# One 128-row operand per head for the attention scores of a fused attention and mixture-of-experts kernel

## The chip, the cores and the metric

The program runs on one core of a Trainium2 chip. A core has a matrix engine (TensorE, PE in the profile, with its weight loads shown apart as PEld), a vector engine (DVE), an activation engine (ACT), a general engine (POOL), and a queue engine (SP) that here only issues DMAs. Each engine works through its own list of instructions in order, and semaphores tie the lists together. The metric is the device time of one execution in microseconds (us), less is better.

## The reference: what is computed

Attention with a decay comes first: 8 batches of 8 heads, 576 positions, 64 features a head. Then each of the 4608 tokens goes through one of 8 experts.

```python
scores = scale * np.matmul(q, k.transpose(0, 1, 3, 2))
cum = np.cumsum(np.log(np.clip(f, 0.0001, 1.0)), axis=-1)
scores = np.where(causal, -1e9, scores + cum[:, :, :, None] - cum[:, :, None, :])
attn = softmax(scores)                      # over the last axis
out = np.matmul(attn, v)                    # -> x, 4608 tokens of 512
e = argmax(x @ w_gate + modality_bias[modality_id])
y = gate_w * (relu(x @ w1[e]) @ w2[e])      # one expert of 8 for each token
```

Since `cum` of the query's row falls out of a softmax, a score needs q·k, minus `cum` of the key, minus a shift of the query (its maximum).

## The kernel before

**Attention.** The 64 heads are worked in 32 pairs `p`. A pair's operands stand together in one tile: the first head's 64 features in partitions 0 to 63, the second's in 64 to 127. To keep f32 accuracy, ACT rounds the loaded features to a shorter format (`split_hi`, L329) and POOL takes the rest (`split_lo`, L335): tile `X` holds both, for keys and queries.

A score group `scores(p, g)` is a sum in PSUM of five kinds of products: a mask (L480, a 128-row product of an identity and a triangle), high keys by high queries, high by low, low by high (all L492 from `X`), and a product of `Sk` and `Sq` (L492 as well), whose few live rows hold the negated cumulated logs of the keys and the shifts of the queries, high and low parts each. All but the mask have 64 rows: the first head's operands in the upper half, the second's in the lower, one matmul for each head, directly one after the other. The four groups of a pair are 288, 288, 448+64 and 320+192 columns wide.

Before that the shift is found. `max_mm` (L419 mask, L424 high by high, L428 `Sk` by the constant `Cq`) makes transposed scores in four groups, DVE reduces them to maxima (L438 to L443), PE transposes the maxima (L449), DVE splits them (L455, L456) and SP writes them into `Sq` with two DMAs (`shift_out`, L463). The logs come into `Sk` with one DMA (`put_cum`, L340). `Sk`, `Sq` and `X` have three buffers each.

Afterwards ACT takes the exponentials (L502) and rounds them (L513), POOL and DVE take the rest (L521), and PE multiplies by the values (`weighted`, L541 to L543, 45 small matmuls a head). DVE divides (L552 to L554), PE transposes (L568) and multiplies by the gate's weights (L584).

**What sets the order.** A class `Plan` orders all steps of the attention before anything is built. Each step has an engine, an assumed cost, the steps that it comes after, buffers that it takes and frees, and a due time: `PER` times its pair plus an entry of the table `DUE`. The planner goes through the steps by greedy choice, and each engine's list is its choice, fixed. The table is a list of numbers; the pairs are staggered by it, so that pair 18's maxima stand beside pair 16's scores. On SP the DMAs stand in one list in this order too.

**Experts.** The second half, from 512 us or so on, sorts tokens by expert and runs full-height matmuls of 128x256 and 128x512 (L1003, L1014); its code is not touched.

## Time and profile before

| what | us |
|---|---|
| median of three timed runs | 1025.76 (1023.96 to 1026.95) |
| the profiled execution | 1013.86 |
| its span, first to last instruction | 1012.1 |
| PE busy | 927.0 (92%) |
| DVE / ACT / POOL busy | 684.1 (68%) / 537.5 (53%) / 361.6 (36%) |

The profiled execution is one run, 1.76 us longer than its span; sums made on its rows are compared with its own time. A row of the timeline has the start and the duration in us, the engine, the source line, the operation with what it writes and reads, its shape (64*128 is a 64-row matmul that uses 128 columns of weights) and a count of merged instructions. Durations of matmuls overlap, so the pace is read from one row's start to the next row's start. A row of windows gives each engine's busy time in a stretch, then the clock granted to PE, as a share of full speed, and the DMA engines' busy share.

### The profile page before, as it was taken

The page shows a single profiled execution, that of the slowest core. Times are in us where ns is not written, and L with a number is a line of the kernel's source. Part 1 is how long each engine was busy: PE and PEld are TensorE (multiplying, and loading weights), DVE is VectorE, ACT ScalarE, POOL GpSimd, SP SyncE. Part 2 cuts the span into 40 slices and gives each one's busy share as a digit, 9 for nine tenths or more (in the row PEclk, how much of TensorE's full clock was granted, in tenths as well). Part 3 has the DMA queues.
Part 4 walks back from the last instruction along what each step waited for, and adds up shares of the span by engine and source line. Part 5 has one row for each costly group of instructions (what it writes and reads, how often), then busy time and mean ns, then how long its engine had stood idle before and what let it go on. Part 6 is the DMA issues. An engine that isn't in the chain of part 4 may idle for free. (4 is left out here: it accounts for less than half of the span.)

```text
span 1012.1 us, 22740 instructions
## 1 busy us (share of the span) xinstructions
PE 927.0 (92%) x9347; PEld 808.8 (80%) x9347; DVE 684.1 (68%) x1173; ACT 537.5 (53%) x655; POOL 361.6 (36%) x278
## 2 busy tenths in 40 slices
PE   5999989999999899979689999999999999999792
PEld 3787778777778777768588999999999999999571
DVE  7867978686777858777547766566666666665382
ACT  2765656655756547547443444445444544544371
POOL 7454556865566474653424311111111110111010
PEclk9897999998999969989779999999999999999796
DMA  5212132332321322212302676111111441124640
GB/s 180 77 50 99 33 126 67 99 99 74 97 78 53 99 84 89 87 57 86 131 33 79 218 256 235 43 43 42 53 43 53 134 139 55 43 84 168 234 161 3
DMA packets 38276, 98.22 MB, mean 97 GB/s; under 512 B 3919, under 2 KB 4559, under 8 KB 38160
## 3 DMA queue, kind: packets, MB, share of 16 engines
q1 hardware_dynamic: 31456, 75.60, 22.5%
q0 software_dynamic: 6704, 21.02, 5.5%
q8 instruction: 79, 1.29, 0.6%
q14 instruction: 37, 0.30, 0.1%
HBM read 133.69 MB, written 21.80 MB: 154 GB/s over the span
## 5 line engine op out<-in xcount | busy, mean ns | idle before, releaser
L521 POOL TENSOR_TENSOR Pl<-Pt,Ph 128x1152 f16<-128x1152 f32 (+1 forms) x64 | 152.3, 2385 | 156.2 <-ACT Ph L513 104.4
L502 ACT ACTIVATE Pt<-ps,lnp 128x1024 f32<-128x1024 f32 (+1 forms) x128 | 117.2, 928 | 112.8 <-PE ps L492 104.8
L1017 POOL DMA_INDIRECT out_dram<-y,xg x36 | 47.4, 1316 | 349.4 <-DVE y L1016 333.1
L1003 PE MATMUL ph<-xh,w1h 128*128 128x256 f32 x576 | 164.3, 286 | 2.0 <-ACT xh L991 1.5
L1003 PE MATMUL ph<-xl,w1h 128*128 128x256 f32 x576 | 164.3, 285 | 0.0
L1003 PE MATMUL ph<-xh,w1l 128*128 128x256 f32 x576 | 164.1, 285 | 0.0
L976 ACT CAST w2h<-raw 128x1024 fp32r<-128x1024 f32 x84 | 86.6, 1050 | 115.1 <-PE py L1014 84.7
L970 DVE TENSOR_TENSOR w1l<-raw,w1h 128x1024 fp32r<-128x1024 f32 x80 | 100.9, 1265 | 58.1 <-ACT w1h L969 57.7
L977 DVE TENSOR_TENSOR w2l<-raw,w2h 128x1024 fp32r<-128x1024 f32 x84 | 100.3, 1221 | 56.5 <-ACT w2h L976 55.2
L969 ACT CAST w1h<-raw 128x1024 fp32r<-128x1024 f32 x80 | 83.3, 1048 | 95.6 <-PE ph L1003 57.8
L492 PE MATMUL ps<-X 64*128 64x288 f32 (+4 forms) x1152 | 125.8, 327 | 0.0
L1014 PE MATMUL py<-w2h,hh 128*128 128x512 f32 x312 | 121.6, 398 | 0.0
L1014 PE MATMUL py<-w2l,hh 128*128 128x512 f32 x312 | 119.7, 391 | 0.7 <-DVE w2l L977 0.7
L1014 PE MATMUL py<-w2h,hl 128*128 128x512 f32 x312 | 119.5, 392 | 0.0
L513 ACT CAST Ph<-Pt 128x1024 f16<-128x1024 f32 (+1 forms) x96 | 103.7, 1082 | 21.3 <-PE po L543 20.3
L1003 PEld LDWEIGHTS ph<-xh,w1h 128*128 128x128 f32 x576 | 111.5, 194 | 3.6 <-ACT xh L991 2.4
L1003 PEld LDWEIGHTS ph<-xl,w1h 128*128 128x128 f32 x576 | 111.7, 194 | 0.7
L541 PE MATMUL po<-vh,Ph 128*128 128x65 f16 x960 | 104.9, 202 | 7.5 <-DVE x L554 7.5
L1003 PEld LDWEIGHTS ph<-xh,w1l 128*128 128x128 f32 x576 | 111.7, 194 | 0.0
L543 PE MATMUL po<-vh,Pl 128*128 128x65 f16 x960 | 104.7, 201 | 5.0 <-issue 3.5
L542 PE MATMUL po<-vl,Ph 128*128 128x64 f16 x960 | 104.8, 200 | 1.8 <-issue 1.8
L492 PEld LDWEIGHTS ps<-X 64*128 64x128 f32 x1152 | 93.1, 196 | 13.2 <-issue 1.8
(253 smaller groups left out, 2025.7 us busy)
## 6 DMA issues: line engine op xcount, KB each, us to landing
raw<-in_w_dram SPq DMA_DIRECT2D x84, 1024.0 KB
raw<-in_qk_dram SPq DMA_DIRECT2D x32, 608.0 KB
xg<-xs SPq DMA_DIRECT2D x20, 514.0 KB
vr<-in_v_dram SPq DMA_DIRECT2D x7, 1024.0 KB
raw1b<-in_w_dram SPq DMA_DIRECT2D x4, 1024.0 KB
hxg<-xs SPq DMA_DIRECT2D x5, 257.0 KB
vr<-in_v_dram SPq DMA_DIRECT2D x2, 512.0 KB
vr<-in_v_dram SPq DMA_DIRECT2D x8, 128.0 KB
```

The costliest lines, as they stand in the source:

```text
L492: nc.tensor.matmul(ps[:, h, c0:c0 + w], a, b, start=(j == 0 and not masked), stop=(j == 3), skip_group_check=True)
L502: nc.scalar.activation(self.get("Pt", (p, i))[:, :, o:o + w], ps[:, :, 0:w], AF.Exp, bias=self.lnp, scale=0.125)
L513: self.nc.scalar.copy(self.Ph_t[p % 2][:, :, c], self.get("Pt", (p, i))[:, :, 0:c.stop - c.start])
L521: e.tensor_tensor(self.Pl_t[p % 2][:, :, c], self.get("Pt", (p, i))[:, :, 0:c.stop - c.start], self.Ph_t[p % 2][:, :, c], ALU.subtract)
L541: nc.tensor.matmul(o, Ph[:, c0:c0 + P], vh[:, c, hh, :], start=(c == 0), stop=False)
L542: nc.tensor.matmul(o[:, 1:65], Ph[:, c0:c0 + P], vl[:, c, hh, :], start=False, stop=False)
L543: nc.tensor.matmul(o, Pl[:, c0:c0 + P], vh[:, c, hh, :], start=False, stop=(c == ic))
L970: nc.vector.tensor_tensor(self.w1l[a], self.raw1[i][a], f32(self.w1h[a]), ALU.subtract)
L976: nc.scalar.copy(self.w2h[a], self.raw2[a])
L977: nc.vector.tensor_tensor(self.w2l[a], self.raw2[a], f32(self.w2h[a]), ALU.subtract)
L1003: nc.tensor.matmul(ph[:, i, :], w[:, k, f0:f0 + P], x[:, k, :], start=(j == 0), stop=(j == len(m) - 1))
L1014: nc.tensor.matmul(py, h[:, k, c * P:c * P + P], w[:, k, :], start=(j == 0), stop=(j == len(m) - 1))
```

## The change

The rows of logs and shifts move into the operand itself. For each head `h` of a pair there is a 128-row operand `A[:, h, :]`: 64 rows are the head's rounded features (the same half of the partitions as before), the other 64 rows hold what stood in `Sk` and `Sq`: ones and cumulated logs on the key side, shifts and ones on the query side. One full-height matmul for each head then does high by high together with the logs and the shift. The two mixed products (high by low, low by high) stay 64-row matmuls. In `max_mm` the shift rows are still zero, and one full-height matmul for each head replaces both 64-row products.

The rounded features are made by ACT for both heads at once in a tile `H` (two copies of 576 columns in place of one of 1216), and go from `H` into the two heads' operands by two DMAs of 64x1280 (new step `cp`, function `put_hi`; for the first pair one ACT and one DVE copy). The logs take two DMAs, and from the fourth pair on two more set the shift rows back to zero; the shift takes four DMAs in place of two. A new function `blank` fills constants into three buffers of `A` at the start. `PER` and `DUE` are other numbers.

```diff
-PER = 13.5
+PER = 12.5
 DUE = {
-    ('setup2',): 36.45, ('hi',): -18.87, ('lo',): -67.23, ('cum',): -14.17, ('mm', 0): -2.46, ('mm', 1): -11.48,
+    ('setup2',): 33.79, ('hi',): -40.67, ('lo',): -86.81, ('cp',): -34.26, ('cum',): 31.87, ('mm', 0): 0.81,
...
+    def blank(self, i, e):
+        A = self.A_t[i]
+        self.nc.gpsimd.memset(f32(self.L_t[i][:, S:QC]), 0.0)
...
+        for h in range(2):
+            o, r = slice(64 - 64 * h, 128 - 64 * h), slice(64 * h, 64 * h + 64)
+            self.nc.gpsimd.memset(f32(A[o, h, S:QW]), 0.0)
+            self.nc.gpsimd.memset(f32(A[r, h, S:QC]), 0.0)
+            for c, m in ((slice(0, S), 0), (slice(QW, XW), 1)):
+                e.tensor_scalar(A[o, h, c], self.ones_f[o].broadcast_to([64, c.stop - c.start]), self.t01[m][o], None, ALU.mult)
...
     def split_hi(self, p):
-        X = self.new(self.qp, "X", p, [P, 2, XW], F32R, 3)
-        self.nc.scalar.copy(X[:, 0], self.get("raw", p))
+        H, raw = self.H_t[p % 2], self.get("raw", p)
+        self.own(("hi", p % 2), p)
+        for x, y in ((H[:, 0:S], raw[:, 0]), (H[:, QC:], raw[:, 1])):
+            self.nc.scalar.copy(x, y)
...
+    def put_hi(self, p):
...
+        H, A = self.H_t[p % 2], self.A_t[p % NX]
+        for h in range(2):
+            r = slice(64 * h, 64 * h + 64)
+            if p:
+                self.nc.sync.dma_start(f32(A[r, h]), f32(H[r]))
+            else:
+                (self.nc.scalar.copy, self.nc.vector.tensor_copy)[h](A[r, h], f32(H[r]))
 
     def put_cum(self, p):
-        self.nc.sync.dma_start(f32(self.Sk[16:P:32, p % 3, 0:S]), f32(self.chl[2 * p:2 * p + 2]))
+        for h in range(2):
+            o = 64 - 64 * h
+            self.nc.sync.dma_start(f32(A[o + 16:o + 64:32, h, 0:S]), f32(self.chl[2 * p + h:2 * p + h + 1]))
+            if p >= NX:
+                self.nc.sync.dma_start(f32(A[o:o + 64:32, h, QW:]), self.zrow)
...
     def max_mm(self, p, g):
-        for c0, w, ic, j0 in segs:
-            for h in range(2):
-                r = slice(64 * h, 64 * h + 64)
-                nc.tensor.matmul(pm[:, h, c0:c0 + w], X[r, 0, QC - 64 + P * ic:QC + 64 + P * ic], X[r, 0, j0:j0 + w],
-                                 start=not masked, stop=False, skip_group_check=True)
-            for h in range(2):
-                r = slice(64 * h, 64 * h + 64)
-                nc.tensor.matmul(pm[:, h, c0:c0 + w], self.Cq[r], self.Sk[r, p % 3, j0:j0 + w], start=False, stop=True,
-                                 skip_group_check=True)
+        for h in range(2):
+            for c0, w, ic, j0 in segs:
+                nc.tensor.matmul(pm[:, h, c0:c0 + w], A[:, h, QC - 64 + P * ic:QC + 64 + P * ic], A[:, h, j0:j0 + w],
+                                 start=not masked, stop=True, skip_group_check=True)
...
     def scores(self, p, g):
+        for h in range(2):
+            for c0, w, c, i0 in segs:
+                k, q = cols(c, w, i0)
+                nc.tensor.matmul(ps[:, h, c0:c0 + w], A[:, h, k], A[:, h, q], start=not masked, stop=False, skip_group_check=True)
         for c0, w, c, i0 in segs:
-            for j, (x, y) in enumerate(((0, 0), (0, 1), (1, 0), (2, 2))):
+            k, q = cols(c, w, i0)
+            for x in range(2):
                 for h in range(2):
                     r = slice(64 * h, 64 * h + 64)
-                    if x < 2:
-                        a, b = X[r, x, k], X[r, y, q]
-                    else:
-                        a, b = self.Sk[r, p % 3, k], self.Sq[r, p % 3, 64 + i0:64 + i0 + w]
-                    nc.tensor.matmul(ps[:, h, c0:c0 + w], a, b, start=(j == 0 and not masked), stop=(j == 3), skip_group_check=True)
+                    a, b = (A[r, h, k], L[r, q]) if x == 0 else (L[r, k], A[r, h, q])
+                    nc.tensor.matmul(ps[:, h, c0:c0 + w], a, b, start=False, stop=(x == 1), skip_group_check=True)
...
+            add("cp", k, "SP" if p else [("ACT", 1.2), ("DVE", 1.2)], 1.1, self.put_hi, k, [("hi", p)] + old, d - 2,
+                lands=655e3 if p else None)
```

Three places of the built lists show how instructions moved. A row has the source line, the operation, what is written and read, the output's size, and a count.

On PE, the maximum's last two groups of a pair (L424 reads the 64-row halves of `X`, L428 the 64-row `Sk`; L419 is the 128-row mask). Before:

```order
L424 MATMUL ps<-X 128x288 x2
L428 MATMUL ps<-Sk,Cq 128x288 x2
L419 LDWEIGHTS ident_162
L419 MATMUL ps<-after,ident_162 128x128
L419 LDWEIGHTS ident_162
L419 MATMUL ps<-after,ident_162 128x128
L424 MATMUL ps<-X 128x288 x2
L428 MATMUL ps<-Sk,Cq 128x288 x2
```

Now, in `max_mm` as well (L458 is the full-height product, L454 the mask, L396 a transpose that belongs to another step):

```order
L458 MATMUL ps<-A_159 128x288 x2
L454 LDWEIGHTS ident_175
L454 MATMUL ps<-after,ident_175 128x128
L454 LDWEIGHTS ident_175
L454 MATMUL ps<-after,ident_175 128x128
L458 MATMUL ps<-A_159 128x288 x2
L396 MATMUL pb<-ident,am 3x128
```

Four products each time became two, and every one of the rows is 128 high.

On PE, a score group of 288 columns. Before (L480 mask, L492 the four products of two heads, L362 another step's transpose):

```order
L480 LDWEIGHTS ident_162
L480 MATMUL ps<-later,ident_162 128x128
L480 LDWEIGHTS ident_162
L480 MATMUL ps<-later,ident_162 128x128
L492 MATMUL ps<-X 128x288 x6
L492 MATMUL ps<-Sq,Sk 128x288 x2
L362 MATMUL pb<-ident,am 3x128
```

Now (L511 mask, L517 full height, L524 the two 64-row kinds):

```order
L511 LDWEIGHTS ident_175
L511 MATMUL ps<-later,ident_175 128x128
L511 LDWEIGHTS ident_175
L511 MATMUL ps<-later,ident_175 128x128
L517 MATMUL ps<-A_159 128x288 x2
L524 MATMUL ps<-L_156,A_159 128x288 x2
L524 MATMUL ps<-A_159,L_156 128x288 x2
```

Eight matmuls became six, two of them full height, and the 64-row ones stand at the group's end.

On SP, one pair's share of the list in the middle of the attention. Before (features L325, logs L340, shifts L463):

```order
L340 DMA Sk<-chl 4x1x576
L325 DMA raw<-in_qk_dram 128x1216
L463 DMA Sq<-mT 2x5x128 x2
L340 DMA Sk<-chl 4x1x576
L325 DMA raw<-in_qk_dram 128x1216
```

Now (copies L362, logs L372, zeros L374, features L338, shifts L495):

```order
L362 DMA A_160<-H_153 64x1280 x2
L372 DMA A_160<-chl 2x1x576
L374 DMA A_160<-zrow 2x640
L372 DMA A_160<-chl 2x1x576
L374 DMA A_160<-zrow 2x640
L338 DMA raw<-in_qk_dram 128x1152
L495 DMA A_159<-mT 1x5x128 x4
L362 DMA A_158<-H_154 64x1280 x2
```

A pair's four DMAs became eleven, and the copy of a pair stands ahead of the shifts of the pair before it.

More of the change, by code (lines that the diff above doesn't have):

```diff
@@ L216, in setup @@
         make_identity(nc, self.ident)
[L217 to L218 removed]
+        self.H_t = [self.qp.tile([P, XW], F32R, name=f"H{i}") for i in range(2)]
+        self.L_t = [self.qp.tile([P, XW], F32R, name=f"L{i}") for i in range(NX)]
+        self.A_t = [self.qp.tile([P, 2, XW], F32R, name=f"A{i}") for i in range(NX)]
+        ones = self.ones_f = t([P, 1], F32, "ones_f")
         nc.gpsimd.memset(ones, 1.0)
[L220 to L225 removed]
+        self.t01 = t0, t1
+        self.zrow = t([2, QW], F32, "zrow")
+        nc.gpsimd.memset(self.zrow, 0.0)
+        self.blank(0, nc.vector)
         self.ident16 = t([P, P], BF16, "ident16")
@@ L458, in shift_out @@
     def shift_out(self, p):
-        self.own(("shift", p % 3), p)
-        mT = self.get("mT", p)
-        for a in range(2):
-            self.nc.sync.dma_start(f32(self.Sq[32 * a:P:64, p % 3, :]), f32(mT[:, a]))
+        self.own(("shift", p % NX), p)
+        mT, A = self.get("mT", p), self.A_t[p % NX]
+        for h in range(2):
+            for a in range(2):
+                r = 64 - 64 * h + 32 * a
+                self.nc.sync.dma_start(f32(A[r:r + 1, h, QW:]), f32(mT[NJ * h:NJ * h + NJ, a]))
     KSEG = [[(0, 288, 0, 0)], [(0, 288, 0, 288)], [(0, 448, 1, 128), (448, 64, 4, 512)], [(0, 320, 2, 256), (320, 192, 3, 384)]]
@@ L469, in scores @@
         nc = self.nc
-        X = self.get("X", p)
-        self.owned(("cum", p % 3), p)
-        self.owned(("shift", p % 3), p)
-        self.owned(("lo", p % 3), p)
+        L, A = self.L_t[p % NX], self.A_t[p % NX]
+        for x in ("cum", "A", "shift", "lo"):
+            self.owned((x, p % NX), p)
         ps = self.new(self.ps_s, "ps", (p, g), [P, 2, 512], F32, 3)
@@ L668, in steps @@
         n, nb = NH * self.nb // 2, self.nb
[L669 removed]
+        plan = Plan(dict(ps=3, pb=1, po=1, Pt=4, raw=2, mt=2, x=2, xT=2, sm=2))
         base = 0.0
```

67 lines of the change are left out of this document (33 added, 34 removed), and 20 rows, old and new, of the table DUE.

## The prediction, as it was put on record

> **What bounds the kernel now.** I read the granted clock and busy times by stage first, then PE's waits, then PE's timeline at full clock. The change touches only the attention, so its stage is what counts. The windows view (a stretch, its length, busy us and instruction counts of PE, PEld, DVE, ACT, POOL, then PE's clock, DMA share, GB/s):
>
> ```profile
> 50.00:500.00 450.00, 410.46 (x5951) 346.84 (x5948) 335.00 (x701) 274.54 (x329) 260.67 (x161) 0.92 0.26 85
> 250.00:300.00 50.00, 47.74 (x744) 40.51 (x743) 35.95 (x84) 33.76 (x40) 29.26 (x20) 1.00 0.27 87
> ```
>
> PE is busy 410.46 of 450 us (91%); DVE comes next with 335.00 (74%). The waits of PE in the same stretch (engine and tile, whom it waited for, total us, times, longest):
>
> ```profile
> PE pb L568 <- DVE lg L590: 9.2, 4, 5.9
> PE po L541 <- DVE x L554: 7.5, 5, 5.1
> PE pb L449 <- DVE roh L615: 4.8, 2, 3.1
> ```
>
> No engine holds PE regularly: these are a few long waits, 21.5 us of the 39.5 us that PE isn't busy, and none is for the shift's or the logs' DMAs. So PE's own list sets the pace, and what a step of PE costs there is paid nearly in full. A busy PE isn't a fast one, so I price by the steps from one row's start to the next. PE's timeline, a stretch at clock 1.00 (start, duration, what):
>
> ```profile
> 252.25 0.33 PE L419 MATMUL ps<-after,ident 128*128 128x64 bf16 x4
> ...
> 253.34 0.20 PE L541 MATMUL po<-vh,Ph 128*128 128x65 f16 x1
> ...
> 254.88 0.40 PE L424 MATMUL ps<-X 64*128 64x288 f32 x2
> 255.12 0.29 PE L428 MATMUL ps<-Sk,Cq 64*128 64x288 f32 x2
> 255.34 0.28 PE L419 MATMUL ps<-after,ident 128*128 128x128 bf16 x2
> 255.56 0.40 PE L424 MATMUL ps<-X 64*128 64x288 f32 x2
> ...
> 256.02 0.38 PE L377 MATMUL pb<-a,ones 1*128 1x1 f32 x2
> ...
> 259.57 0.20 PE L541 MATMUL po<-vh,Ph 128*128 128x65 f16 x1 [0.61 <-DVE x L554]
> ...
> 260.93 0.39 PE L419 MATMUL ps<-after,ident 128*128 128x128 bf16 x4
> 261.24 0.36 PE L424 MATMUL ps<-X 64*128 64x192 f32 x2
> ...
> 261.96 0.34 PE L480 MATMUL ps<-later,ident 128*128 128x128 bf16 x4
> ...
> 263.61 0.28 PE L480 MATMUL ps<-later,ident 128*128 128x128 bf16 x2
> 263.83 0.67 PE L492 MATMUL ps<-X 64*128 64x288 f32 x6
> 264.33 0.29 PE L492 MATMUL ps<-Sq,Sk 64*128 64x288 f32 x2
> 264.46 0.60 PE L492 MATMUL ps<-X 64*128 64x288 f32 x6
> 264.86 0.32 PE L492 MATMUL ps<-Sq,Sk 64*128 64x288 f32 x2
> 265.12 0.66 PE L568 MATMUL pb<-ident,x 128*128 128x128 f32 x4
> 265.61 0.39 PE L480 MATMUL ps<-later,ident 128*128 128x128 bf16 x4
> ...
> 267.14 0.34 PE L419 MATMUL ps<-after,ident 128*128 128x64 bf16 x4
> ```
>
> Two things are to be seen. First, two 64-row matmuls of the two heads run together: three pairs of 288 columns take 264.46 to 264.86, 0.133 us a pair. Second, going between 128-row and 64-row work costs extra, in three places. Into it: four masks take 0.31 us (260.93 to 261.24) and two take 0.22 (255.34 to 255.56), so a mask is 0.045 and the passage 0.13. At the first pair: three pairs right behind masks take 0.50 (263.83 to 264.33) instead of 0.40, so 0.10. Out of it: a pair followed by a 128-row instruction takes 0.22 (255.12 to 255.34) instead of 0.13, so 0.09. One 64-row block costs about 0.3 us beyond its products.
>
> **The change part by part.** *Maxima.* Now, for a pair of heads: 1.09 us (252.25 to 253.34), 1.14 (254.88 to 256.02) and 1.03 (260.93 to 261.96), in all 3.26. After the change everything there is 128 rows high. The trace has full-height matmuls of rounded f32 in the experts' half, each with new weights, and narrow ones at the gate:
>
> ```profile
> 599.93 0.28 PE L1003 MATMUL ph<-xh,w1l 128*128 128x256 f32 x1
> 600.05 0.28 PE L1003 MATMUL ph<-xh,w1h 128*128 128x256 f32 x1
> ...
> 605.45 0.39 PE L1014 MATMUL py<-w2l,hh 128*128 128x512 f32 x1
> 605.68 0.40 PE L1014 MATMUL py<-w2h,hl 128*128 128x512 f32 x1
> ```
>
> ```profile
> 483.89 1.26 PE L584 MATMUL pb<-wg,xT 128*128 128x8 f32 x10
> 485.01 0.38 PE L480 MATMUL ps<-later,ident 128*128 128x128 bf16 x4
> ```
>
> 256 columns take 0.12 us, 512 take 0.23; on that line 288 columns take 0.134, 320 0.148, 448 0.203. However narrow, a matmul with 128x128 f32 weights takes 0.11 (ten in 483.89 to 485.01), which I take for 192 and 64. A full-height matmul thus costs what a *pair* of 64-row ones does, and the products don't get cheaper: one head's six widths (64, 448, 192, 320, 288, 288) come to 0.84 us, both heads to 1.68, where before two products of a pair came to the same. Only the passages go. With ten masks (0.5) the maxima cost 2.18 us, 1.08 less.
>
> *Scores.* Now 1.65 us (261.96 to 263.61), 1.51 for the two groups of 288 (263.61 to 265.12), 1.53 (265.61 to 267.14): 4.69. After: full-height products 1.68, two mixed kinds as pairs 1.68, masks 0.5, and a 64-row block in each of four groups, 1.2: 5.06, so 0.37 more, since the two groups of 288 shared one block and no longer do. Net 0.71 us a pair of heads, 23 us for 32. A second way: the built lists have 231 such blocks before and 128 after; 103 times 0.3 is 31 us. The first way bounds it below, the second above, and I take 26.
>
> That is at full clock. At the stage's 0.92 it is 28; of that I count the 91% in which PE isn't waiting: 26.
>
> *Weight loads.* The row that could speak against full height is the weight load's own:
>
> ```profile
> L1003 PEld LDWEIGHTS ph<-xh,w1h 128*128 128x128 f32 x576 | 111.5, 194 | 3.6 <-ACT xh L991 2.4
> ```
>
> A load lasts 194 ns on average, yet the matmuls come 0.12 us apart, each with its own load, so loads hide behind the matmul before. The Trainium skill, page "TensorE: Matmul & The Clock Gate", Part 3, says that weight loads overlap with matmuls in flight only when their row groups differ, which full-height operands' never do; its load time of 128/1.2 ns, 107 ns, over 768 new full-height matmuls would by my estimate add 82 us. The spacing of 0.12 us here disagrees with that rule, so nothing is added.
>
> *Copies, logs, shifts.* SP's issues and what they bring; the first row is a line's instructions (ns: least, median, most), the others are from the timeline:
>
> ```profile
> L463 SPq DMA_DIRECT2D Sq<-mT x46: 497/512/540, 102.8 to 427.2; - x46
> ```
>
> ```profile
> 9.30 0.70 SPq L340 DMA_DIRECT2D Sk<-chl  x1
> ...
> 12.37 0.34 SPq L325 DMA_DIRECT2D raw<-in_qk_dram  x1
> ```
>
> ```profile
> 11.32 0.53 PE L428 MATMUL ps<-Sk,Cq 64*128 64x192 f32 x2 [2.52 <-DMA Sk<-chl]
> ```
>
> ```profile
> 16.46 1.21 ACT L329 CAST X<-raw 128x1216 fp32r<-128x1216 f32 x1 [7.12 <-DMA raw<-in_qk_dram]
> ```
>
> A small DMA's data are used 2.0 us after its issue (9.30 to 11.32), 608 KB after 4.1 us (12.37 to 16.46). Eleven issues of some 0.5 us are 5.6 us of SP for a pair, every 15 us: room. A copy of 640 KB can start once the scores of three pairs earlier are done and is then ready after about 5 us; in the new list PE meanwhile has three heads of values (1.36 us each, 259.57 to 260.93), three maximum groups (2.18), a score group (1.5) and the gate's work, over 9 us. That hides it; without cover it would cost 32 times 5 us. The shift's rows come 1.0 us later (two more issues at 0.51): hidden too, more narrowly, see the slower rival. ACT's two short copies replace one of 1.20 us and POOL's two halves replace one: counted as nothing, both engines being busy for 61% and 58%.
>
> *Start.* DVE's constants:
>
> ```profile
> 5.11 1.50 DVE L224 TENSOR_SCALAR Sk<-ones_f,t 128x576 fp32r<-128x576 f32 x1
> ...
> 8.04 0.45 DVE L237 TENSOR_SCALAR chl<-Pt 64x576 fp32r<-64x576 f32 x1
> ```
>
> Four such fills for the first operand cost 1.8 to 6 us (four at 0.45, four at 1.50) against some 2.7 that leave, and the first pair's copy by ACT and DVE adds about 1.2 to its chain. Ends: 0 and 4.5 us; I take 2, nearer to DVE's row of 64 partitions. The fills of the other two operands go to POOL, which is idle for 42% of the stage after.
>
> *Sum.* Saved 26; start 2 back; and 3 back as waits, because a PE that arrives earlier meets DVE's x and lg later in its own list (a seventh of the 21.5 us above). Net 21 us: the profiled execution of 1013.86 us would be 993. That execution was 11.9 us under the median of the timed runs, so the median goes from 1025.76 to 1005.
>
> **The rivals.** *Turned into waits:* PE gets shorter, but DVE or ACT now hold it, and 4 us or less remain: 1022. For it: pairs are staggered, and ACT and DVE work in between. Against it: DVE has 335.00 us for 30 pairs of heads, 11.2 a pair, against some 15 for PE.
>
> *Slower, by shifts that land late:* in SP's list the four shift DMAs stand behind the next pair's copy, logs and features. From the transposed maxima to that pair's first scores PE has two score groups of the pair before (1.65 and 0.75), a head of values (1.36), two maximum groups (1.5), a transpose (0.5) and one more group (0.75): 6.5 us. The chain is a transpose and a split (0.8), four issues (2.0), 2.0 to land: 4.8, under 6.5. If the copy's or the features' 4.1 us are still on the DMA engines, it is 8.9, a wait of 2.4. In every pair that is 77 us, in half of them 38: with 21 saved, 17 slower, 1043. It decides from a wait of 0.66 us a pair on. For it: DMA share is only 0.26 now, but copies add 640 KB a pair to 608. Against it: the copy is issued some 10 us before.
>
> *More than forecast, by the clock:* 0.92 over 450 us means 72 us at half speed. Should an evener PE list halve it, 18 us more go: 987. It may as well grow.
>
> *Weight loads in the open:* full height can't load ahead; by the row of 194 ns over 768 matmuls 149 us more, less 21: 1154. The 0.12 us spacing speaks against it, and so against the page named above.
>
> **How the numbers follow.** Forecast, 1005 (its own range 993 to 1017): 0.59. Turned into waits: 0.14. Late shifts: 0.13. Clock: 0.12. Weight loads: 0.02. 0.3% is 3.1 us, about what a measurement of this kernel tells from no change. Faster by more: the forecast, the clock and a third of the waits rival, 0.76; within: 0.09, the rest of that rival; slower: 0.15. The range leaves a tenth at each end: from 984, past the clock's case, to 1030, into the late shifts' case.
>
> **What would show it.** Right: maxima near 2.2 us a pair, no gap beyond mask spacing ahead of full-height rows, score groups of 288 at about 0.85 to 0.95 us each, and the experts' first matmuls some 20 us earlier. Wrong: PE rows of scores that wait for the shift's DMA, full-height rows of 288 columns much over 0.134 us apart, a stage clock far from 0.92, or PE waits over 60 us in the stage.

## The result, and the profile after

The changed kernel is slower: 1054.46 us median (1052.84 to 1055.73) against 1024.86 us (1020.63 to 1026.95) for the kernel before on the same chip, a ratio of 1.029 (95% interval 1.026 to 1.033). The prediction was 1005 us, on the other side. The profiled execution has a span of 1054.0 us where it had 1012.1; the experts' first matmul starts at 552.4 us instead of 512.5, and from there to the end it is 501.6 us against 499.6. So the 40 us were lost in the attention. Ratios here and below compare the fast executions alone: one that took over 1.5% more than the fastest of the same kernel is left out.

The windows view of the kernel after (busy us and counts of PE, PEld, DVE, ACT, POOL, then PE's clock, DMA share, GB/s), its first 50 us and the stage that the prediction rests on:

```profile
0.00:50.00 50.00, 19.56 (x104) 15.12 (x104) 28.69 (x55) 17.79 (x24) 37.04 (x81) 0.76 0.45 131
50.00:500.00 450.00, 387.77 (x4715) 333.27 (x4714) 334.02 (x651) 254.36 (x326) 257.76 (x173) 0.85 0.41 114
```

and the first 50 us of the kernel before:

```profile
0.00:50.00 50.00, 37.29 (x357) 28.73 (x358) 38.80 (x69) 25.14 (x27) 29.43 (x61) 0.93 0.40 129
```

PE is busy for less time in the stage (387.77 us, before 410.46) although it got through less of its list, and at a lower clock: 0.85, before 0.92. Both are signs of an engine that waits. Worked out from the clock records and the gaps between PE's rows, from the first weighted matmul to the experts' first: idle 41.5 us before and 67.7 after, time at half clock 80.3 and 136.5. PE's waits after (engine and tile, whom it waited for, total us, times, longest):

```profile
PE pb L411 <- DVE a L405: 22.9, 6, 4.3
PE ps L458 <- DMA A<-H: 8.7, 1, 8.7
PE pb L600 <- DVE rr L670: 8.0, 6, 1.3
```

The first has no counterpart before and comes six times, once per batch of four pairs: PE's third matmul of the value scale waits for the second reduction (L405). DVE's timeline at one of these places (start, duration):

```profile
109.54 0.20 DVE L622 TENSOR_TENSOR lg<-pb,lg 128x40 f32<-128x40 f32 x1 [2.58 <-PE pb L616]
...
110.01 0.20 DVE L634 TENSOR_TENSOR rd<-lg,rm 128x40 f32<-128x40 f32 x1
110.24 2.00 DVE L638 TENSOR_SCALAR rc<-rd 128x40 f32<-128x40 f32 x1
112.28 1.36 DVE L639 TENSOR_TENSOR rc<-rc,iota_e 128x40 f32<-128x40 f32 x1
113.68 0.20 DVE L642 TENSOR_REDUCE rei<-rc 128x5 f32<-128x40 f32 x1
113.91 1.10 DVE L644 TENSOR_TENSOR roh<-iota_e,rei 128x40 f32<-128x40 f32 x1
...
115.14 2.15 DVE L694 TENSOR_SCALAR rse<-rse 128x5 f32<-128x5 f32 x1
...
117.77 0.14 DVE L405 TENSOR_REDUCE a<-pb 1x1 f32<-1x3 f32 x1
```

and POOL's beside it:

```profile
107.69 4.52 POOL L553 TENSOR_TENSOR Pl<-Pt,Ph 128x1152 f16<-128x1152 f32 x2
112.17 2.78 POOL L352 TENSOR_TENSOR L<-raw,H 128x576 fp32r<-128x576 f32 x2
114.91 2.36 POOL L553 TENSOR_TENSOR Pl<-Pt,Ph 128x1152 f16<-128x1152 f32 x1
```

The expert routing of the batch before stands ahead of L405 in DVE's list. Its operations have 5 or 40 columns and cost some 0.2 us when POOL is idle, but three of them last until a POOL row ends: L638 ends at 112.24 and POOL's row at 112.21, L644 at 115.01 and POOL at 114.95, L694 at 117.29 and POOL at 117.27. A fourth, L639, ends at 113.64, where the first of the two operations in POOL's middle row ends (113.59). Over the whole run L694 took 2.15 to 2.22 us in the six batches in which POOL was busy beside it, and 0.17 in the two in which it was not. So 0.14 us of value scale waits behind over 7 us of routing.

PE's own work, at full clock (the step from one row's start to the next row's):

```profile
100.84 0.33 PE L454 MATMUL ps<-after,ident 128*128 128x64 bf16 x4
101.70 0.40 PE L454 MATMUL ps<-after,ident 128*128 128x128 bf16 x4
102.51 0.60 PE L600 MATMUL pb<-ident,x 128*128 128x128 f32 x4
102.86 0.51 PE L517 MATMUL ps<-A 128*128 128x288 f32 x2
103.30 0.40 PE L524 MATMUL ps<-L,A 64*128 64x288 f32 x2
...
103.76 0.40 PE L511 MATMUL ps<-later,ident 128*128 128x128 bf16 x4
...
105.33 0.28 PE L479 MATMUL pb<-ident,mt 128*10 128x128 f32 x1
105.44 0.33 PE L511 MATMUL ps<-later,ident 128*128 128x128 bf16 x4
...
107.07 0.33 PE L600 MATMUL pb<-ident,x 128*128 128x128 f32 x1
107.24 0.28 PE L511 MATMUL ps<-later,ident 128*128 128x128 bf16 x2
...
108.22 1.28 PE L616 MATMUL pb<-wg,xT 128*128 128x8 f32 x10
```

```profile
87.79 0.50 PE L458 MATMUL ps<-A 128*128 128x288 f32 x2
...
88.23 0.51 PE L458 MATMUL ps<-A 128*128 128x288 f32 x2
88.58 0.34 PE L454 MATMUL ps<-after,ident 128*128 128x64 bf16 x4
```

Two maximum groups take 0.86 (100.84 to 101.70) and 0.81 us (to 102.51), the third 0.79 (87.79 to 88.58): 2.46 us a pair, before 3.26. The score groups take 0.90 (102.86 to 103.76), 1.57 (to 105.33), 1.63 (105.44 to 107.07) and 0.98 (107.24 to 108.22): 5.08, before 4.69. The operand does save PE work, 0.41 us a pair, 13 us in all; the loss is elsewhere.

Last, the start. POOL's rows there, then SP's, then PE's:

```profile
18.04 3.71 POOL L266 TENSOR_SCALAR A<-ones_f,t 64x576 fp32r<-64x576 f32 x2
...
22.25 3.58 POOL L266 TENSOR_SCALAR A<-ones_f,t 64x576 fp32r<-64x576 f32 x2
...
32.25 5.92 POOL L352 TENSOR_TENSOR L<-raw,H 128x576 fp32r<-128x576 f32 x4
```

```profile
24.60 10.76 SPq L338 DMA_DIRECT2D raw<-in_qk_dram  x2
35.45 3.10 SPq L495 DMA_DIRECT2D A<-mT  x4
```

```profile
29.91 0.38 PE L396 MATMUL pb<-ident,am 128*3 128x128 f32 x1 [6.04 <-DVE am L388]
...
39.67 0.61 PE L517 MATMUL ps<-A 128*128 128x320 f32 x1 [5.92 <-DMA A<-mT]
```

The fills of constants hold POOL until 26 us; its remainder of pair 1, the first two of the four operations in the last row, ends at 35.0; the load of pair 3's features waits for it at the head of SP's queue (the row of 10.76 us, which ends at 35.4), and the first pair's shifts stand behind that load. The first weighted matmul starts at 58.5 us, before at 45.1. So 13.4 of the 40 us were lost by then, and 26.5 between there and the experts, about what PE's idle time grew by (26.2).

### The profile page after: what moved, and what is told of

The parts are those of the page before. It is cut to its first block, busy times and chain, and to the rows that moved or that the text cites. A ratio compares the mean times of both kernels' runs of the same rounds, so it can differ in the third digit from the quotient of the medians.

```text
span 1054.0 us, 21733 instructions
## 1 busy us (share of the span) xinstructions
PE 922.2 (87%) x8579; PEld 813.8 (77%) x8579; DVE 702.0 (67%) x1176; ACT 542.7 (51%) x688; POOL 390.3 (37%) x331
## 5 line engine op out<-in xcount | busy, mean ns | idle before, releaser
L553 POOL TENSOR_TENSOR Pl<-Pt,Ph 128x1024 f16<-128x1024 f32 (+1 forms) x64 | 151.5, 2378 | 98.0 <-ACT Ph L545 92.0
L1052 POOL DMA_INDIRECT out_dram<-y,xg x36 | 45.1, 1252 | 345.6 <-DVE y L1051 320.9
L534 ACT ACTIVATE Pt<-ps,lnp 128x576 f32<-128x576 f32 (+1 forms) x128 | 116.5, 929 | 104.1 <-PE ps L524 100.8
L352 POOL TENSOR_TENSOR L<-raw,H 128x576 fp32r<-128x576 f32 x62 | 99.6, 1628 | 85.9 <-PE ps L524 85.3
L458 PE MATMUL ps<-A 128*128 128x288 f32 (+4 forms) x384 | 95.8, 368 | 22.4 <-DMA A<-chl 11.3
```

Source lines behind the costliest of these rows:

```text
L352: e.tensor_tensor(L[:, c], y, f32(H[:, c]), ALU.subtract)
L458: nc.tensor.matmul(pm[:, h, c0:c0 + w], A[:, h, QC - 64 + P * ic:QC + 64 + P * ic], A[:, h, j0:j0 + w], start=not masked, stop=True, skip_ ...
L534: nc.scalar.activation(self.get("Pt", (p, i))[:, :, o:o + w], ps[:, :, 0:w], AF.Exp, bias=self.lnp, scale=0.125)
L553: e.tensor_tensor(self.Pl_t[p % 2][:, :, c], self.get("Pt", (p, i))[:, :, 0:c.stop - c.start], self.Ph_t[p % 2][:, :, c], ALU.subtract)
```

## The experiments

Chips differ: the kernel before took 1004 to 1029 us in the six sets of runs told of here, so each run is given with its ratio to the kernel before in the same set, with a 95% interval. The changed kernel itself took 1054.46 us on one chip and 1055.88 on another.

**Which half of the change?** The table of due times and the operand came together, so each was run without the other. The changed structure with the old table:

```diff
-PER = 12.5
+PER = 13.5
 DUE = {
-    ('setup2',): 33.79, ('hi',): -40.67, ...
+    ('setup2',): 36.45, ('hi',): -18.87, ... ('cp',): -16.0,
```

> The new operand with the old order numbers (PER 13.5 and the old DUE table, the new step cp given -16.0, just behind the rounding). Theory A (the changed kernel loses by its order: routing steps on DVE stand in front of the value-scale chain, PE idles 4 us a batch and falls to half clock; and by its start): the steady part gains some 12 us of PE time, the start of some 10 to 16 us stays: 1020 to 1035. Rival B (the operand itself costs the time, by its copies, four shift DMAs and SP's longer list): 1045 to 1060 whatever the order, with waits of PE for A<-H or A<-mT in every pair.

1056.83 us, 1.029 (1.023 to 1.034): in time rival B, but without its sign. PE waited for `A<-H` and `A<-mT` four times in all, for 12.0 us, and for the value scale's second reduction 1.2 us. And the old structure with the new table, the reverse of that diff on the kernel before:

> The old operand (X, Sk, Sq, Cq as before) with the new order numbers. Theory A: most of the steady loss comes along with the numbers: 1040 to 1060, with PE waits for the reduction of the value scale and half-clock stretches once a batch. Rival B: near the kernel before, 1020 to 1030.

1060.81 us, 1.030 (1.020 to 1.039): in time about what theory A expected, but without its sign, since PE waited only 0.6 us for the value scale's second reduction (L371). Either half alone costs as much as both. The longest waits of this last run:

```profile
PE pb L449 <- DVE mt L438: 9.3, 3, 6.4
PE po L541 <- DVE x L554: 8.0, 7, 4.5
```

They are at other places than in the changed kernel, for other operations. So the loss is no cost of the operand plus a cost of the table: added up, the two would have come to twice as much. A table that fits only the work it was made for would explain the two halves, but not that the new table with the new work is slow as well; that is taken up below.

**The two visible waits, one at a time.** The fills as memsets, and the memset of `vr` ahead of them:

```diff
-                e.tensor_scalar(A[o, h, c], self.ones_f[o].broadcast_to(...), self.t01[m][o], None, ALU.mult)
+                self.nc.gpsimd.memset(f32(A[o, h, c]), float(m))
+                for r in range(o.start, o.stop, 32):
+                    self.nc.gpsimd.memset(f32(A[r:r + 1, h, c]), 1.0 - m)
```

> The changed kernel with the constants of the second and third operand filled by POOL memsets instead of POOL products, and the clearing of vr's last rows moved ahead of them. Theory A: the start's 16 us (first score matmul at 39.7 us against 23.5) go back by 10 to 14, all of it seen at the end: 1040 to 1045. Rival (the early pairs only wait elsewhere, since the later order catches up): 1051 to 1056.

1058.73 us, 1.031 (1.025 to 1.037): nothing gained. PE's wait between 20 and 50 us, and SP's queue:

```profile
PE ps L522 <- DMA A<-mT: 12.6, 1, 12.6
```

```profile
25.24 11.05 SPq L343 DMA_DIRECT2D raw<-in_qk_dram  x2
36.38 3.10 SPq L500 DMA_DIRECT2D A<-mT  x4
```

The waits of 6.04 us for DVE and 5.92 for the shifts became one of 12.6 for the shifts, still behind the load that waits for POOL's remainder. Then the routing steps of each batch were spread behind the next value scale:

```diff
-            for s in self.steps(early).order():
+            for s in self.spread(self.steps(early).order()):
```

> The changed kernel, its order kept but for the routing steps on DVE of each batch (all after the first), which no longer stand ahead of the next value scale's reductions but behind them, one in every four steps. Theory A: the 3.3 to 4.3 us that PE waits in each of six batches go, and with them most of the half-clock stretches of 14 to 24 us behind them: 20 to 40 us less, 1015 to 1035. Rival C (PE would idle anyway, as the steps just get late for something else): 1048 to 1056, with the same half-clock time near 130 us in the attention.

1059.11 us, 1.029 (1.019 to 1.039). The wait got another name, a DVE operation further on:

```profile
PE pb L600 <- DVE x L586: 22.7, 6, 4.1
```

22.7 us in place of 22.9: the work on DVE had only been moved. In both runs theory A failed and the rival came, with times 3 us above its range.

**Taking work away.** So the next edits make the lists shorter instead of permuting them. The routing:

```diff
-            nc.vector.tensor_scalar(c, self.get("rd", b), 0.0, 8.0, ALU.is_lt, ALU.mult)
-            nc.vector.tensor_tensor(c, c, self.iota_e, ALU.add)
+            nc.vector.scalar_tensor_tensor(c, self.get("rd", b), -1e30, self.iota_e, ALU.mult, ALU.add)
...
-            nc.vector.tensor_scalar(se, se, 1e-9, None, ALU.add)
```

> The changed kernel with two of VectorE's routing steps of each batch taken out without changing a number of the output: the addition of 1e-9 (line 694, 2187 ns each in the changed kernel) is left out because the sum it goes onto is at least 1, and lines 638 and 639 (1657 and 1359 ns) become one operation. Theory A (VectorE is what TensorE waits for at each batch's end, because short routing operations there last as long as GpSimd's operation beside them): the waits for the value scale, 22.9 us between 50 and 530 us, fall under 10 us, the half-clock time falls with them, and the time comes to 1025-1042 us. Rival B (something else comes right behind, so the wait only changes its name): sum of TensorE's waits in the stage as before, 1050-1060 us.

1036.48 us, 1.026 (1.019 to 1.032), in theory A's range, though the changed kernel itself was not run on this chip. The wait at the value scale fell:

```profile
PE pb L411 <- DVE a L405: 8.1, 6, 1.7
```

The start, with the fills of above and four steps moved:

```diff
+            for name, after in ((("setup2",), ("lo", 1)), (("cum", 2), ("so", 0)), (("raw", 2), ("cum", 2)), (("raw", 3), ("raw", 2))):
+                s = next(x for x in out if x["name"] == name)
+                out.remove(s)
+                out.insert(1 + next(i for i, x in enumerate(out) if x["name"] == after), s)
```

> The changed kernel with the start alone altered: the fills of constants as memsets, the shifts of pair 0 sent ahead of the cumulated logs of pair 2 and the loads of pairs 2 and 3, and GpSimd's remainder of pair 1 ahead of its second group of constants. Theory A: the first score product starts near 25 us instead of 39.67, the first weighted matmul near 46-50 us instead of 58.5, and the whole time falls by that, to 1041-1048 us. Rival B: pairs 1 and 2 then wait for their own operands (their copies and remainders come no earlier), the first weighted matmul stays after 55 us and the time within 5 us of 1054.

1049.07 us, 1.037 (1.031 to 1.044), a microsecond outside theory A; the first weighted matmul at 50.6 us. Both together:

> Both edits, the start's and the routing's. If they are two separate losses they add up: 1012-1032 us, at or below the kernel before. If one idle place only hands its time to the next (rival B), above 1045 us.

1027.56 us, 1.015 (1.009 to 1.022). These three ran on one chip, so their medians compare: the start is worth 8.9 us (1036.48 to 1027.56), the routing 21.5 (1049.07 to 1027.56), inside the range expected of the sum, but still above the kernel before. The routing's edit on the kernel before:

> The kernel before with the routing edit alone (its line 606 is 1068 ns, 607 734 ns, 662 172 ns each). Theory A: there these operations stand ahead of nothing that TensorE waits for except some transposes (9.9 us in 100:480), so 1017-1027 us. Rival: any time off VectorE helps whatever the order, then 1005-1015 us.

1002.00 us, 0.994 (0.990 to 0.998): some 6 us, by its ratio theory A. The edit is worth over three times as much to the changed kernel. Where the operations stand in DVE's list need not be the reason, since there they also last longer. One of them between 100 and 480 us, first before, then in the changed kernel:

```profile
L662 DVE TENSOR_SCALAR rse<-rse 128x5 f32<-128x5 f32 x7 | 1.2, 172 | 0.2
L694 DVE TENSOR_SCALAR rse<-rse 128x5 f32<-128x5 f32 x6 | 13.1, 2187 | 0.2
```

Over the whole run the routing's rows that write `rd`, `rc`, `roh` and, from itself, `rse` fell from 46.4 to 28.6 us of DVE by the edit to the changed kernel (with the start's edits, for 21.5 us), and from 23.5 to 19.1 by the edit to the kernel before (for some 6): both gains are a little more than the DVE time taken off.

**Queues, and the clock.** For one chip's comparison the changed kernel ran again:

> The changed kernel itself, so that the edits of this set and the kernel before are compared with it on one chip: 1.025 to 1.040 times the kernel before.

1055.88 us, 1.050 (1.044 to 1.057), above the expected range: its time was that of the first chip, while the kernel before was 20 us faster here. Then two more waits were taken out (the last kernel's 4.5 us for a row of ones and 9.1 us for copies, which stood on SP behind loads of sorted tokens):

```diff
-        for t in range(2):
-            self.load_x(t)
...
+                if s["name"] == ("raw", 31):
+                    late()
```

> The start's and the routing's edits together, and two more that take a wait out of a queue: GpSimd's row of ones ahead of its fills (the first value scale waited 4.5 us for it), and the first two loads of sorted tokens on the queue of SP behind the copies of pair 30 instead of ahead of them (TensorE waited 9.1 us for those copies). Theory A: 1.027 times the kernel before less 13.6 us of waits and some half clock, 1.000 to 1.008 times the kernel before on the same chip. Rival B (the waits come back elsewhere): 1.012 to 1.020.

1029.92 us, 1.025 (1.019 to 1.031): 26 us better than the changed kernel on that chip, but no better than without these two edits (1027.56 us on another chip): rival B, and beyond its range. Two waits of 4.1 and 3.6 us, for ACT and for DVE, had come in their place. To price the half clock, matmuls nobody reads were put into the waits:

```diff
+        pv = self.get("pb", ("v3", b))
+        for i in range(36 if b else 0):
+            nc.tensor.matmul(pv[:, 256:384], self.ident16, self.after, start=True, stop=True)
         pv = self.bank(("v2", b))
```

> The changed kernel with matmuls whose result nobody reads, put where TensorE waits at each batch's end: 36 of 128 columns ahead of the matmul that waits for the value scale (line 411) and 12 ahead of the transposes of line 600. They take about the time of the waits (3.8 and 1.3 us a batch), so they cost TensorE next to nothing, and VectorE is late as before. Theory D (about half of the loss is the half clock that follows TensorE's idle spells): the half-clock time between the first weighted matmul and the experts falls from 136 us to 80-105, and the time by 10 to 25 us. Rival E (the half clock comes from something else, such as the sum of the work, and the idle time is the whole loss): half-clock time and time within 5 us of the changed kernel, or longer.

1064.87 us, 1.063 (1.054 to 1.071). They didn't do what was meant:

```profile
186.21 4.00 PE L412 MATMUL pb<-after,ident 128*128 128x128 bf16 x36 [3.33 <-DVE a L405]
```

They write the bank that L405 reads, so they wait with everyone and then run 4.00 us at half clock. Useless work of 4.8 us a batch cost 9 us in all, while half-clock time fell from 127.5 to 83.3 us. On the kernel with the two queue edits, with fewer of them:

> The last kernel with 16 and 12 such matmuls ahead of the two waits of each batch, now 1.7 and 1.3 us long. Theory D: half-clock time falls by a further 20 to 40 us and the time by 5 to 15 us, to 0.988-1.002 times the kernel before. Rival E: no change against the last kernel, or 2 to 5 us longer.

1026.60 us (1018.15 to 1030.21), 1.024 (1.017 to 1.030), where the same kernel without them took 1029.92. Half-clock time fell from 118.7 to 47.0 us in the profiled execution, whose 1018.15 us was also the fastest of its four. The clock granted over a whole execution rose in all four, to 0.937 to 0.950 from 0.917 to 0.932, and the other three still took 1025.10 to 1030.21 us: no change in the median that can be told, as rival E had it. The clean test fills the idle spell with products by zero that wait for nothing late:

```diff
+        if g == 0 and p % 4 == 3 and p < 31:
+            for i in range(50):
+                nc.tensor.matmul(pm[:, 1, 384:512], self.zero16, self.later, start=False, stop=True, skip_group_check=True)
```

> The changed kernel with TensorE's idle spell at each batch's end filled: 50 matmuls of 128 columns that add zeros to the maxima's tile of pair 4b+3, right ahead of the matmul that waits for the value scale (line 411, 3.8 us a batch). Unlike the matmuls of the run with 36 and 12, which turned out to wait for the same VectorE operation and ran behind it (4.0 us a batch at half clock), these wait for nothing that is late; at 66 ns each, as such matmuls took in that kernel's successor at full clock, they last 3.3 us. Theory D (the half clock behind idle spells is a large part of the loss): the wait falls below 1 us a batch, half-clock time from 127-136 us to under 95, time 1035-1046 us. Rival H (VectorE and GpSimd pace the batch, TensorE's clock only fills their time): half-clock time falls but the time stays within 5 us of 1055.

1056.31 us, 1.027 (1.023 to 1.031), with these rows in its profile:

```profile
PE pb L413 <- DVE a L407: 5.5, 5, 1.5
```

```profile
50.00:500.00 450.00, 403.98 (x5245) 350.30 (x5246) 337.22 (x662) 258.75 (x331) 259.04 (x175) 0.90 0.41 115
```

The clock rises from 0.85 to 0.90, half-clock time falls to 89.7 us, and the time stays: rival H. The profiled execution, 1050.91 us, is the fastest of its five; over all five the granted clock was 0.922 to 0.940, where eight executions of the changed kernel on two other chips had 0.908 to 0.923. Read so, the slow clock here mostly filled time that PE would have spent waiting: a sign of the loss more than its cause. The test leaves room for some 8 us, though: the filling took 24.0 us in seven batches, and idle time fell by 16.2.

**Fitting the order.** What was left was the order itself. The planner works with a duration for each step, and the table's were not the chip's: scores 0.85 + 0.7 + 1.45 + 1.45 = 4.45 us a pair where the trace has 5.08, issue of logs 2.0 where four SP rows take 3.3, of shifts 2.0 where four take 3.0, routing steps 0.4 to 0.6 where 1.4 to 2.4 was put in (L638 and L639 alone took 3.36 us above). SP's rows for the logs and the shifts of one pair in the changed kernel:

```profile
439.84 2.98 SPq L495 DMA_DIRECT2D A<-mT  x4
...
444.17 0.94 SPq L372 DMA_DIRECT2D A<-chl  x1
445.17 1.35 SPq L374 DMA_DIRECT2D A<-zrow  x1
446.57 0.48 SPq L372 DMA_DIRECT2D A<-chl  x1
447.10 0.48 SPq L374 DMA_DIRECT2D A<-zrow  x1
```

For the kernel before the same list says 4.70 for the scores, and the trace 4.69. So the durations were corrected, the planner was told when each engine is free at the start, and the due times were searched anew, with no other edit:

```diff
-PER = 12.5
+PER = 28.15
...
-        done, ef, dma = {}, dict.fromkeys(self.LAT, 0.0), 0.0
+        done, ef, dma = {}, dict(PE=0.0, ACT=0.0, DVE=3.0, POOL=20.3, SP=3.2), 0.0
...
-                add("s", k + (g,), "PE", (0.85, 0.7, 1.45, 1.45)[g], self.scores, (p, g), ...
+                add("s", k + (g,), "PE", (1.0, 0.9, 1.64, 1.56)[g], self.scores, (p, g), ...
-            add("cum", k, "SP", 2.0 if p >= NX else 1.0, self.put_cum, k, old, d - 4, lands=20e3)
+            add("cum", k, "SP", 3.3 if p >= NX else 1.1, self.put_cum, k, old, d - 4, lands=20e3)
-            add("rt", k + (1,), "DVE", 0.4, self.route, (b, 1), [("rt", b, 0)], e + 1)
+            add("rt", k + (1,), "DVE", 2.4, self.route, (b, 1), [("rt", b, 0)], e + 1)
```

> The changed kernel with nothing altered but the order: the table of due times fitted anew, with the durations that the trace of the changed kernel shows put in place of the table's own (scores 1.0, 0.9, 1.64 and 1.56 us where the table has 0.85, 0.7, 1.45 and 1.45; cumulated logs 3.3 us of issue where it has 2.0; shifts 3.0 where it has 2.0; the routing steps 1.4, 2.4 and 2.0 where it has 0.4, 0.4 and 0.6). Theory F (the order was made for durations that the chip does not give): idle time of TensorE between the first weighted matmul and the experts falls from 69 to under 45 us, half-clock time from 127-136 to under 90, time 1010-1035 us. Rival G (the operand costs this time in any order): above 1045 us.

1016.32 us, 0.988 (0.985 to 0.992): faster than the kernel before, and 38 to 40 us under the changed kernel's medians on two other chips (40 under the filled kernel's on this one), by order alone. Theory F, though idle time stayed at 57.6 us where under 45 was expected. Its stage, and its longest waits:

```profile
50.00:500.00 450.00, 401.65 (x5362) 350.88 (x5362) 346.94 (x703) 277.57 (x359) 268.41 (x180) 0.92 0.43 123
```

```profile
PE pb L533 <- DVE lg L676: 14.7, 2, 7.4
PE po L629 <- POOL Pl L607: 13.7, 5, 6.4
```

The value scale no longer waits, the clock is back at 0.92, half-clock time is 85.3 us and the experts start at 508.5 us, 44 earlier. The start came back too, with the fills as they were: the first weighted matmul stands at 43.6 us. Whether the corrected durations did this, or a new search as such, was not tried: no run has a new search with the old durations. The fit on top of the fills, the shorter routing and the two queue edits:

> The same fit of the order on top of the faster fills, the shorter routing, the early row of ones and the later loads of sorted tokens (1029.92 us with the old order). Theory F: idle time under 30 us, half-clock time under 70, time 975-1000 us, faster than the kernel before. Rival G: above 1015 us.

1009.01 us, 0.977 (0.971 to 0.984): faster, but 9 us short of theory F's range, with 35.0 us of idle time and 92.2 at half clock. The kernel before with the shorter routing and a fit of its own, in the same set:

> The kernel before with the shorter routing and its own table fitted anew in the same way (its table's scores, 0.95, 0.7, 1.55 and 1.5 us, already sum to the 4.69 us that its trace shows; routing and VectorE's remainders are corrected). It is the yardstick for the fit: if fitting is worth the same to both kernels, it takes 25-40 us off here too (965-985 us where the kernel before takes 1005-1010) and the new operand is still no gain; if the kernel before was already fitted (theory F), 3 to 12 us beyond the shorter routing's 0.994 times.

1008.35 us, 0.981 (0.976 to 0.987), some 1.3% beyond the shorter routing alone, a little over theory F's 3 to 12 us. And the kernel before with a fitted table and the routing as it was:

> The kernel before with nothing altered but its order, fitted in the same way as the order of the changed kernel that came to 0.988 [0.985, 0.992] times the kernel before. The two stand side by side then: old operand and new operand, each with an order fitted to its own durations and no other edit. If the operand is worth the 12 us that its shorter maxima and longer scores give (0.39 us times 32 pairs), this one comes to 0.996-1.003; if it is worth nothing once the order fits, 0.982-0.994.

1017.80 us, 1.004 (0.998 to 1.010), above both ranges. It doesn't show what a fit of its own is worth to the kernel before: its `PER` and all 64 entries of its `DUE` are the ones of the run before, number for number, while the routing and two of the planner's durations for it differ, so one search served both. On this chip the kernel before spread from 1005 to 1030 us, too, and against the median of all its 19 executions there, 1021.65 us, the ratio is 0.996. What stands is that a fit took some 4% off the changed kernel (1.029 to 0.988) and 1.3% or less off the kernel before. Last, the version that came to 0.977 with POOL's constants held back at the start, which has a newly searched table as well:

> The changed kernel with the start's edits, the shorter routing and a fitted order as in the run that came to 0.977 times the kernel before, with GpSimd's second group of constants held behind its remainder of pair 1 (TensorE waited 6.6 us for that remainder there, and 7.3 us for copies). If the start was what was left: 0.960-0.974. If the waits only move: 0.974-0.985.

1006.27 us, 0.990 (0.985 to 0.995), and 0.985 against that median: faster than before, and short of the range for a start that was what was left. By its ratio it is behind the version without that edit and by its time ahead of it; on two chips and with two tables, that does not decide it.

What the operand is worth by itself isn't settled. With a fitted order and no other edit the new operand stands at 0.988 and the old, with a table taken over, at 1.004 (0.996 by the other median), so 0.8 to 1.6% better, where its 13 us of PE work are 1.3%. With the shorter routing and, on the new operand's side, the start's edits, they stand at 0.977 and 0.981 on one chip, which can't be told apart. Each fit is one outcome of a search, and another one may land a few us elsewhere. Nothing to some 16 us is what these runs point to, and their intervals allow more on both sides.

## Why the prediction was wrong

*What bounds the kernel.* Right of the kernel before: PE's list set its pace. The step that failed took this over to the changed kernel: "3 back as waits", a seventh of the waits that stood in the trace of before. A wait isn't a property of two operations but of an order, and the order was new. In place of those 3 us, idle time rose by 26 us behind the first weighted matmul, and half-clock time by 56; PE's busy time there stayed at 426 us, so the 13 us of saved work don't show at the slower clock. The fit of the order, with no change to the work, took some 38 us off the time again. That the order was at fault is thereby shown; why it fitted so badly is argued from the durations below. The covers for copies and shifts were read off the new order; what DVE has to do ahead of the value scale was not added up, nor were the planner's durations set against the trace, where the scores alone (4.45 against the prediction's own 5.06) would have shown that the order was made for another PE.

*Maxima and scores.* The sign was right and the size off: net 0.41 us a pair, not 0.71. Maxima were forecast at 2.18 and took 2.46, scores at 5.06 and took 5.08. What was mis-sized is "only the passages go": two full-height matmuls of 288 columns behind masks take 0.35 us together (88.23 to 88.58), not 0.268. The upper bound, 0.3 us for each of 103 blocks, rests on that error: part of what I had priced as the passage into 64-row work is paid by these full-height f32 matmuls behind the bf16 masks too: the first of the two takes 0.22 us to the next one's start, the second 0.13.

*Weight loads.* Right: no load in the open. That rival's 149 us are 4.7 us a pair (24 loads of 194 ns); maxima and scores came to 7.54 us a pair where 7.24 was forecast.

*Copies, logs, shifts.* Right for the steady stage in that no wait for a shift is among its longest; two rows were missed. Near the end a copy stood on SP behind loads of sorted tokens (the wait of 8.7 us for `A<-H`), and at the start the shifts stood behind a load.

*Start.* Forecast 2 us; the first weighted matmul came 13.4 us later, and the edits of the start gave 8.9 us back. The sentence that failed is that the fills "go to POOL, which is idle for 42% of the stage after": they run before that stage, when DVE, SP and through them PE wait for POOL. Their price was taken from DVE's rows; on POOL a fill of 64 x 576 takes 1.8 us. Yet the fills alone are not the cost: with the same fills and a fitted order the first weighted matmul came at 43.6 us.

*The rivals.* None named the cause. "Turned into waits" had the right mechanism with a price of 4 us or less gained; it could not go below zero because it took waits to be what PE's saving turns into. "Late shifts" had the right sign by a wait that came once, at the start (5.92 us), and not in the steady stage. "Clock" counted the gain and had the loss in one sentence, "it may as well grow": it did, but as the filling run shows, mostly as a companion of the waits.

*What would show it wrong.* Two of the signs came in full: the stage clock of 0.85, and PE waits over 60 us in the stage (450 less 387.77 is 62). A third came in part: full-height rows of 288 columns stand 0.22 us apart right behind masks and 0.13 elsewhere.

## What to carry to other kernels

A change to the work under an order fitted by hand or by search is two changes, and here the second was the larger: before pricing the work, set the durations that the order was made with against the trace, and after the change fit the order again before judging the operand. Count what stands in an engine's list ahead of each step that another engine waits for, in durations as they are beside their neighbours, not as they are alone. A wait that is moved comes back under another name (22.9 us became 22.7); work taken off the list that PE waits for (17.8 us in eight batches) took 21.5 us off the time.

## What was not expected of the hardware

- **VectorE operations last as long as GpSimd's operation beside them.** A 128x5 addition took 2.15 us and two operations of 128x40 took 2.00 and 1.10, each ending within 0.06 us of GpSimd's row; the addition took 0.17 us in the two batches in which GpSimd was idle. Reductions (L642) and operations that read PSUM (L622) in the same stretch took 0.20. The Trainium skill, page "VectorE: DVE Perf Modes", section "Two Vector instructions with no wait between them", names a second read interface that VectorE shares with GpSimd, used by operations with two SBUF tensor inputs and by those in a two-port mode. The trace agrees for L639 and L644, which have two SBUF inputs and were held; the mode of L638 and L694, with one, is not in it. That they are held to the end of GpSimd's instruction is read off this trace's rows. L634, with two SBUF inputs as well, took 0.20 us in the same stretch: it started at 110.01, just ahead of the end of a GpSimd operation at 110.08, and in another batch it took 2.18 us, to within 0.05 us of the end of one.
- **Half clock costs little where PE waits anyway.** 38 to 47 us less of it left the time unchanged (1054.46 and 1055.88 us without the filling, 1056.31 with it, on three chips; ratios 1.029, 1.050 and 1.027). The filling matmuls of 128 columns stood 105 ns apart at half clock (the 36 in 4.00 us) and, in the other filled kernel, 56 at full (the 12 in 0.83 us of the row below).

```profile
239.66 0.83 PE L608 MATMUL pb<-after,ident 128*128 128x128 bf16 x12 [0.50 <-DVE rrk L673]
```

- **The chips differ for one kernel and not for the other.** The kernel before took 1024.86 and 1004.39 us on two chips, the changed kernel 1054.46 and 1055.88 on the same two. Why the waiting kernel doesn't gain on the faster chip was not tried.
